# Second mixture of a fused attention and two-mixture kernel: the third token tile of each expert gathered and transposed as full 128 rows, its transposes in one run behind the first down products, the matmul order written out

## The chip, the cores and the metric

The kernel runs on one core of a Trainium2 chip. The metric is device microseconds (us) of one execution; lower is better.

## The reference

Attention over 2 x 8 heads of 576 tokens gives x (1152 tokens by 512). A first mixture of 8 experts weighs every expert for every token. The second mixture, where the change is, sends each token to its two best experts:

```python
def _moe2_ref(x, w_gate, w_noise, noise, w1, w2):
    noisy_logits = x @ w_gate + np.log1p(np.exp(x @ w_noise)) * noise
    top2 = np.argpartition(-noisy_logits, 2, axis=1)[:, :2]
    ...                       # top2_w: softmax over the two
    for e in range(E):        # E = 8, D = 512, F = 1024
        for k in range(2):
            mask = top2[:, k] == e
            h = np.maximum(x[mask] @ w1[e], 0.0)
            out[mask] += top2_w[mask, k, None] * (h @ w2[e])
```

## The kernel before

Every fp32 operand of a large product is split into a rounded high part and a low rest (`split`: ScalarE writes the high part, VectorE the rest), and each product is three matmuls (`mm3`, L164): high by high, high by low, low by high.

Routing on the chip writes, for each expert, a table of token rows. Expert 0 is handled within the routing code. The other seven are ordered by how many tokens they got, and `expert(i)` for i = 0 to 6 takes the i-th. It has room for CAPS[i] = 344, 320, 312, 304, 298, 292, 288 tokens: two tiles of 128 and a third of 88, 64, 56, 48, 42, 36, 32 rows (`sizes`). Table slots that no token took hold the numbers of the zero rows ahead of the tokens. Above that room a branch at the end would take the rest; it isn't taken here.

In `expert(i)`, in program order:

- `fetch(i + 1)`: three gathers of the next expert's token rows from HBM, one per tile, by indirect DMAs of GpSimd (`pull`, L563), into five buffers `xg`.
- `up`: for each of 8 blocks of hidden units 12 matmuls into a PSUM tile `h` (L164, in the traces h<-xh,wh and the like, as wide as the expert's room; 96 in all), then `split` into `hh` and `hl`. Where the third tile has at most 64 rows (i = 1 to 6, "short"), its hidden values go unsplit into `tail`.
- Loading and converting the weights: both halves of this expert's w2 (`vs`: the first into a `wh`/`wl` buffer, the second into `xwh`/`xwl`), both halves of the next expert's w1 (`ws`). The buffers `wh`/`wl` are three. For a short expert the raw w2 lies in `acc`.
- `prep`: the next expert's tokens are transposed on TensorE (L750, `xgt<-cs,xg`). There are four steps, one per quarter of the 512 features; a step transposes a 128-feature block of all three tiles side by side into one PSUM tile of tag "b" (two buffers), and `split` moves it to `xh` and `xl` (ACT L104, DVE L106). The third tile's transpose takes k rows of `xg` and k rows and columns of the unit matrix.
- The down products: `part(j, h)` of the class `Down` is tile j by half h of w2: 12 matmuls `y<-wh,hh` and the like, 512 wide (L164). A tile's two parts add up in one PSUM tile of tag "a" or "c"; after part 1 ScalarE scales it (L820), and GpSimd adds it to the output by an indirect DMA (L824). For a short expert the third tile goes through `tail` (L838): unsplit fp32 matmuls `y<-acc,tail` that put pieces of the output side by side in the PSUM partitions. In the traces each of them is two records, 32 in all for i = 1 to 5.

For expert(0) to expert(5) the scheduler of the kernel's language chooses where TensorE's instructions stand (it keeps what depends on each other in order). Expert 0, the routing and expert(6) stand under `manual_schedule`, so that TensorE takes them as they are written. ScalarE, VectorE and the queues are scheduled by the language in all of expert(0) to expert(6).

The tokens of expert(0) are transposed at the end of the routing code by the same `prep_steps`, a step after every sixth matmul of expert 0's last tile (`between`, `down(vs, [late], ...)`).

Of the kernel before, what the change touches and what calls it, by code (L numbers as in the profile page):

```python
# [19 lines left out]
N, DM, E, F = B * S, H * D, 8, 1024  # L20
# [42 lines left out]
def tile_kernel(ctx: ExitStack, tc: tile.TileContext, qL, kL, vL, qS, kS, vS, wg, u12, w1, w2, wgn, noise, v1, v2, cst, masks, dummy, out):  # L63
    nc = tc.nc
# [9 lines left out]
    def ps(tag, name):  # L74
        return psum.tile([128, 512], F32, tag=tag, name=name)
# [9 lines left out]
    ident = cs[:, C_ID:C_ID + 128]  # L85
# [13 lines left out]
    def split(hi, lo, src, relu=False):  # L99
        if relu:  # L100
            seen[0] = nc.scalar.activation(hi, src, AF.Relu)  # L101
            nc.vector.scalar_tensor_tensor(lo, src, 0.0, hi.bitcast(F32), op0=ALU.max, op1=ALU.subtract)  # L102
        else:
            seen[0] = nc.scalar.activation(hi, src, AF.Copy)  # L104
            firsts.append(seen[0])
            nc.vector.tensor_tensor(lo, src, hi.bitcast(F32), op=ALU.subtract)  # L106

    def fetch_w(src, raw=None):
        if raw is None:
            raw = rpool.tile([128, 4, 512], F32, tag="raw", name="raw")  # L110
        nc.sync.dma_start(raw, src)
        return raw

    def conv_w(raw, spare=False, pool=False):
        if spare:
            hi, lo = (xpool.tile([128, 4, 512], F32R, tag=t, name=t, bufs=1) for t in ("xwh", "xwl"))
        else:
            hi, lo = (wpool.tile([128, 4, 512], F32R, tag=t, name=t, bufs=3) for t in ("wh", "wl"))
        if pool:
            for s in range(4):  # L120
                nc.scalar.activation(hi[:, s], raw[:, s], AF.Copy)
                nc.gpsimd.tensor_tensor(lo[:, s], raw[:, s], hi[:, s].bitcast(F32), op=ALU.subtract)
            return hi, lo
        for s in range(2):
            split(hi[:, 2 * s:2 * s + 2], lo[:, 2 * s:2 * s + 2], raw[:, 2 * s:2 * s + 2])
        return hi, lo

    def load_w(src, spare=False):
        return conv_w(fetch_w(src), spare)
# [6 lines left out]
    def conv_u2(raw):  # L136
        hi, lo = (upool.tile([128, 2, 512], F32R, tag=t, name=t) for t in ("u2h", "u2l"))
        split(hi, lo, raw)
        return hi, lo

    def conv_u1(raw):
        hi, lo = (upool.tile([128, 7, 2, 128], F32R, tag=t, name=t) for t in ("u1h", "u1l"))
        v = raw.rearrange("p c (j n) -> p j c n", j=2)
        for j in range(2):
            split(hi[:, 2 * j:2 * j + 2].rearrange("p a b n -> p (a b) n"),
                  lo[:, 2 * j:2 * j + 2].rearrange("p a b n -> p (a b) n"), v[:, j])
        return [[[x[:, 2 * j + c // 2, c % 2] for c in range(NC)] for j in range(2)] for x in (hi, lo)]

    def conv_wino(raw):
        hi, lo = (upool.tile([128, 7, 2, 128], F32R, tag=t, name=t) for t in ("u1h", "u1l"))  # L150
        t = upool.tile([128, 4, 2, 128], F32, tag="ut", name="ut", bufs=1)
        b11, b21, b12, b22 = (raw[:, 2 * k:2 * k + 2, j * 128:(j + 1) * 128] for j in range(2) for k in range(2))
        for o, x, y in ((0, b12, b11), (2, b22, b12), (1, b22, t[:, 0]), (3, b21, t[:, 1])):
            nc.gpsimd.tensor_tensor(t[:, o], x, y, op=ALU.subtract)  # L154
        split(hi[:, :2].rearrange("p a b n -> p (a b) n"), lo[:, :2].rearrange("p a b n -> p (a b) n"), raw[:, :, :128])
        split(hi[:, 2], lo[:, 2], b22)
        split(hi[:, 3:], lo[:, 3:], t)
        return hi, lo
# [389 lines left out]
    def total(m=None):  # L548
        p = ps("b", "cnt")
        nc.tensor.matmul(p[:, :E], onesb, cnt, start=True, stop=m is None)  # L550
        if m is not None:
            for i in range(RB):
                nc.tensor.matmul(p[:, :E], onesb, m[:, i], start=False, stop=i == RB - 1)
        return p

    def gather(row, n, rows=PAD + N):
        tt = gpool.tile([128, 2], I32, tag="tt", name="tt", bufs=3)
        nc.sync.dma_start(tt[:n], table[ds(row, n), :])
        return tt, pull(tt, n, rows)

    def pull(tt, n, rows=PAD + N):
        xg = gpool.tile([128, DM], F32, tag="xg", name="xg", bufs=5)
        nc.gpsimd.indirect_dma_start(out=xg[:n], out_offset=None, in_=x2d[:rows, :],  # L563
                                     in_offset=bass.IndirectOffsetOnAxis(ap=tt[:n, 0:1], axis=0))
        return xg
# [31 lines left out]
    for q in range(NP):  # L597
        raw = fetch_u(0, q)
        with tc.issue_after(firsts[min(q, 1) * 3 + 8].ins):
            a, b = conv_u1(raw[0]), conv_u2(raw[1])  # L600
# [28 lines left out]
    for q in range(NP):  # L629
        q = NP - 1 - q  # L630
        if q < NP - 1:
            raw = fetch_u(0, q)
            a, b = conv_u1(raw[0]), conv_u2(raw[1])
# [73 lines left out]
    for e in range(1, E - 1):  # L707
        for q in range(NP):
            raw = fetch_u(e, q)
            a, b = conv_wino(raw[0]), conv_u2(raw[1])  # L710
            for u in range(2):
                x = Unit(a, u)
# [30 lines left out]
    def prep_steps(xgs, ns, c0, bank="b"):  # L743
        n = sum(ns)

        def step(c):
            p = ps(bank, "xgt")
            o = 0
            for xg, k in zip(xgs, ns):
                nc.tensor.transpose(p[:, o:o + k], xg[:k, c * 128:(c + 1) * 128], ident[:k, :k])  # L750
                o += k
            split(xh[:, c, c0:c0 + n], xl[:, c, c0:c0 + n], p[:, :n])

        return [partial(step, c) for c in range(NC)]

    def prep(xgs, ns, c0):
        for step in prep_steps(xgs, ns, c0):
            step()

    def hid(x, f, o, n):  # L760
# [85 lines left out]
    def down(ws, tts, ns, o, last=False):  # L846
        d = Down(ws, tts, ns, o)
        order = [(j, h) for j in range(len(ns)) for h in range(2)]
        if not last:
            order.sort(key=lambda x: x[1])  # L850
        for j, h in order:
            d.part(j, h)
# [5 lines left out]
    def sizes(i):  # L858
        return 128, 128, CAPS[i] - FULL
# [8 lines left out]

    def fetch(i):
        tts = [lists[i][:, j] for j in range(3)]  # L870
        return [(t, pull(t, k)) for t, k in zip(tts, sizes(i))]

    def weights(w, e, h):
        return w[ds(e, 1), h].rearrange("o p c n -> (o p) c n")
# [47 lines left out]
    raws = fetch_w(w1[0, 1]), fetch_w(w2[0, 1])  # L922
    ORDERED = {mybir.EngineType.PE, mybir.EngineType.DVE, mybir.EngineType.Activation}
    with tc.manual_schedule(engines=ORDERED):
# [6 lines left out]
        raws = [fetch_w(v1[0, h]) for h in range(2)]  # L931
# [32 lines left out]
        got = [gather(o, 128, PAD + 768) for o in range(0, EARLY, 128)]  # L964
        g2(*b0, (6, 7), e, False)
        p = total()
# [3 lines left out]
        ws = [conv_w(raws[0])]  # L970
# [3 lines left out]
        raws = [fetch_w(v2[0, h]) for h in range(2)]  # L974
# [7 lines left out]
        vs = [conv_w(raws[0])]  # L982
# [14 lines left out]
        raws = [fetch_w(weights(v1, order[0], 0))]  # L997
# [17 lines left out]
        ws = new  # L1015
# [4 lines left out]
        got = got1  # L1020
# [6 lines left out]
    def expert(i, ws, got):  # L1027
        n, last = CAPS[i], i == E - 2
        k = n - FULL
        short = k <= 64  # L1030
        cur = got
        if not last:
            got = fetch(i + 1)
        tail = gpool.tile([128, 8, 64], F32, tag="tail", name="tail") if short else None
        up(ws, (i + 1) % 3 * 384, 0, n, banks="dac", tail=tail)
        raws = [fetch_w(weights(v2, order[i], h), acc[:, 4 * h:4 * h + 4] if short else None) for h in range(2)]
        vs = [conv_w(raws[0]), conv_w(raws[1], True)]
        if not last:
            ws = [load_w(weights(v1, order[i + 1], h)) for h in range(2)]
            prep([x for _, x in got], sizes(i + 1), (i + 2) % 3 * 384)  # L1040
        tts = [t for t, _ in cur]
        if not short:
            down(vs, tts, sizes(i), 0, last)
            return ws, got
        d = Down(vs, tts[:2], (128, 128), 0)
        d.part(0, 0)
        d.part(1, 0)
        d.tail(raws, tail, tts[2], k)
        d.part(0, 1)
        d.part(1, 1)  # L1050
        return ws, got

    for i in range(E - 2):
        ws, got = expert(i, ws, got)
    most = nc.values_load(bigi, min_val=0, max_val=4 * ROWS)
    with tc.manual_schedule(engines={mybir.EngineType.PE}):
        expert(E - 2, ws, got)

    with tc.If(most > 0):
        with tc.For_i(0, E, 1) as e:  # L1060
            begin = nc.values_load(ovr[:1, ds(e, 1)], engines=(mybir.EngineType.SP,), min_val=0, max_val=E * ROWS - NOVER * OVER)
            with tc.For_i(0, NOVER, 1) as r:
                tt, xg = gather(begin + r * OVER, OVER)
                prep([xg], [OVER], 0)
                ws = [load_w(weights(w, e, h)) for w in (v1, v2) for h in range(2)]
                up(ws[:2], 0, 0, OVER)
                down(ws[2:], [tt], [OVER], 0)
# [82 lines left out]
```

## Time and profile before

| | |
|---|---|
| time, median of 3 runs | 1117.54 us (1116.22 to 1119.85) |
| profiled execution: its own time, the span | 1120.2 us |
| TensorE matmuls busy | 1102.6 us, 98% of the span |
| VectorE / ScalarE / GpSimd busy | 665.0 / 394.3 / 173.8 us |
| start of expert(0) to expert(6) in the chain that ended last | 892.39 us |

For the profiled execution the span is the one time that is listed; nothing is listed around it. A matmul's record lasts longer than its share of TensorE, since matmuls overlap. A busy share of 98% therefore does not say that the engine runs at its best rate. That is read from the starts, or from the chain of work that ended last, whose pieces follow each other without a gap.

### The profile page before, as it was taken

Reading aid. Unit: us, or ns where it says so; the run is one execution under the profiler, and the core shown is the slowest. Engines: PE = TensorE matmul, PEld = TensorE weight load, DVE = VectorE, ACT = ScalarE, POOL = GpSimd, SP = SyncE. Lnnn points to the kernel's source line nnn. Section 1 sums busy time; section 2 is a strip of 40 time slices with the busy share of each in tenths; the row PEclk is TensorE's granted clock in tenths of the full one; section 3 lists DMA queues with packets and bytes.
Section 4 is the critical chain, followed back from the end, with each engine's and each line's share of the span. In section 5 each row is a group of like instructions: output and inputs, shape, how many; then the busy total and the mean of one; then the engine's idle time right before and its main releaser. Section 6 shows DMA issues by size and latency. Waiting matters only on the chain.

```text
span 1120.2 us, 17350 instructions
## 1 busy us (share of the span) xinstructions
PE 1102.6 (98%) x6878; PEld 957.3 (85%) x6878; DVE 665.0 (59%) x1374; ACT 394.3 (35%) x884; POOL 173.8 (16%) x204
## 2 busy tenths in 40 slices
PE   9899999999999999999999999999999999999996
PEld 5677989899998999899999989998888888888885
DVE  5785697666666666666666767553366364544440
ACT  5542144333332333323333323231123263544441
POOL 2110022111112111121111110000041431322211
PEclk9899999999999999999999999999999999999999
DMA  9512135112111121111111111022113682555541
GB/s 278 151 57 75 38 103 159 38 38 75 39 38 38 39 76 38 38 39 38 45 69 38 38 39 56 20 75 75 47 49 88 174 303 41 197 196 194 170 102 23
DMA packets 31216, 96.27 MB, mean 86 GB/s; under 512 B 6522, under 2 KB 15226, under 8 KB 22556
## 3 DMA queue, kind: packets, MB, share of 16 engines
q1 hardware_dynamic: 16028, 78.13, 20.6%
q0 software_dynamic: 5200, 10.17, 4.3%
q10 hardware_dynamic: 9904, 6.83, 2.0%
q8 instruction: 55, 0.90, 0.3%
q14 instruction: 29, 0.24, 0.1%
HBM read 83.60 MB, written 11.60 MB: 85 GB/s over the span
## 4 chain that ended last, share of the span: by engine, by line
PE 87%; DVE 4%; issue 3%; DMA 3%; POOL 2%; ACT 1%; POOLq 0%; ACTq 0%; SPq 0%
PE y L164 40%; PE h L164 16%; PE a L665 14%; PE b L665 7%; PE d L665 3%; PE y L838 2%; PE xgt L750 1%; DMA table<-en,si 1%; PE sc L225 1%; POOL table L498 1%; PE sc L210 1%; PE tr L241 1%; DMA wg_sb<-in_wg 1%; PE ot L247 1%; DMA xg<-x2d,tt 1%
## 5 line engine op out<-in xcount | busy, mean ns | idle before, releaser
L591 DVE SCALAR_TENSOR_TENSOR acc<-y,P,acc 128x512 f32<-128x512 f32 x207 | 152.6, 748 | 141.7 <-PE y L164 141.7
L164 PE MATMUL y<-u2h,gh 128*128 128x512 f32 x504 | 198.3, 394 | 0.3 <-DVE acc L591 0.3
L164 PE MATMUL y<-u2l,gh 128*128 128x512 f32 x504 | 197.1, 391 | 0.0
L164 PE MATMUL y<-u2h,gl 128*128 128x512 f32 x504 | 189.9, 392 | 0.7 <-DVE gl L102 0.6
L154 POOL TENSOR_TENSOR ut<-raw 128x256 f32<-128x256 f32 x48 | 35.6, 762 | 513.2 <-DVE u1l L106 442.0
L164 PEld LDWEIGHTS y<-u2h,gl 128*128 128x128 f32 x504 | 94.3, 188 | 20.9 <-DVE gl L102 2.0
L164 PE MATMUL h<-xl,wh 128*128 128x384 f32 (+8 forms) x352 | 110.2, 313 | 0.0
L164 PE MATMUL h<-xh,wh 128*128 128x384 f32 (+8 forms) x352 | 109.6, 315 | 0.3 <-DVE hl L102 0.3
L164 PE MATMUL h<-xh,wl 128*128 128x384 f32 (+8 forms) x352 | 109.8, 312 | 0.0
L164 PEld LDWEIGHTS y<-u2h,gh 128*128 128x128 f32 x504 | 94.7, 188 | 15.4 <-issue 0.7
L164 PEld LDWEIGHTS y<-u2l,gh 128*128 128x128 f32 x504 | 94.6, 188 | 13.9
L101 ACT ACTIVATE hh<-h 128x256 fp32r<-128x256 f32 (+2 forms) x88 | 35.5, 415 | 97.8 <-PE h L164 97.7
L164 PEld LDWEIGHTS h<-xh,wh 128*128 128x128 f32 x352 | 66.2, 189 | 2.1 <-DVE hl L102 0.6
L164 PEld LDWEIGHTS h<-xl,wh 128*128 128x128 f32 x352 | 66.4, 189 | 1.1 <-issue 0.6
L104 ACT ACTIVATE u2h<-raw 128x1024 fp32r<-128x1024 f32 x31 | 32.8, 1059 | 96.2 <-PE y L164 96.2
L164 PEld LDWEIGHTS h<-xh,wl 128*128 128x128 f32 x352 | 66.3, 188 | 0.0
L102 DVE SCALAR_TENSOR_TENSOR hl<-h,hh 128x256 fp32r<-128x256 f32 (+2 forms) x88 | 40.4, 464 | 38.9 <-ACT hh L101 38.9
L106 DVE TENSOR_TENSOR wl<-raw,wh 128x1024 fp32r<-128x1024 f32 x42 | 49.6, 1221 | 18.7 <-ACT wh L104 18.7
L665 PE MATMUL b<-sh,u1h 128*128 128x288 f32 x192 | 56.9, 296 | 0.0
L665 PE MATMUL a<-sh,u1l 128*128 128x288 f32 x192 | 56.9, 296 | 0.0
L665 PE MATMUL b<-sl,u1h 128*128 128x288 f32 x192 | 56.8, 296 | 0.0
L665 PE MATMUL a<-sl,u1h 128*128 128x288 f32 x192 | 56.7, 295 | 0.0
(248 smaller groups left out, 2502.5 us busy)
## 6 DMA issues: line engine op xcount, KB each, us to landing
raw<-in_u SPq DMA_DIRECT2D x31, 1024.0 KB, 5.0
raw<-in_v SPq DMA_DIRECT2D x20, 1024.0 KB, 10.3
acc<-in_v SPq DMA_DIRECT2D x12, 1024.0 KB, 7.5
raw<-in_w SPq DMA_DIRECT2D x4, 1024.0 KB, 5.3
out<-zero ACTq DMA_DIRECT2D x1, 3072.0 KB, 18.7
x2d<-acc ACTq DMA_DIRECT2D x9, 256.0 KB, 2.0
vs<-in_vL SPq DMA_DIRECT2D x4, 432.0 KB, 11.4
ks<-in_kS SPq DMA_DIRECT2D x4, 297.0 KB, 7.7
```

The costliest lines, as they stand in the source:

```text
L101: seen[0] = nc.scalar.activation(hi, src, AF.Relu)
L102: nc.vector.scalar_tensor_tensor(lo, src, 0.0, hi.bitcast(F32), op0=ALU.max, op1=ALU.subtract)
L104: seen[0] = nc.scalar.activation(hi, src, AF.Copy)
L106: nc.vector.tensor_tensor(lo, src, hi.bitcast(F32), op=ALU.subtract)
L154: nc.gpsimd.tensor_tensor(t[:, o], x, y, op=ALU.subtract)
L164: nc.tensor.matmul(o, a, b, start=start, stop=stop)
L210: nc.tensor.matmul(o, onesb, onesb[:, None, :].to_broadcast([128, 4, 128]), start=True, stop=True)
L225: nc.tensor.matmul(sc[h * 64:h * 64 + w, i * nk:(i + 1) * nk], qs[r, j * w:(j + 1) * w], ks[r, j * step:j * step + nk], start=False, stop= ...
L241: nc.tensor.transpose(tr[:nk, i * nq:(i + 1) * nq], s[:, i], ident[:nq, :nq])
L591: nc.vector.scalar_tensor_tensor(acc[:, t], p, P[:, t, scale:scale + 1], acc[:, t], op0=ALU.mult, op1=ALU.add)
L665: nc.tensor.matmul(p, l[:, b, c], m, start=first and i == 0, stop=i == 5, skip_group_check=not first)
L838: nc.tensor.matmul(p[j * w:j * w + k, :d], hr[:, f, :k], raws[f // 4][:, f % 4, j * d:(j + 1) * d], start=f == 0, stop=f == 7)
```

## The change

Each expert now gathers 128 rows for its third tile and transposes all of them; of the transposed columns only the first k are split and used, as before. Expert(0) to expert(5) stand in written order on TensorE too. In `expert`, `prep` comes behind the first down part, with its four quarters in PSUM tags b, b, d, d, so that twelve transposes stand in a row; behind them comes `tail` for a short expert, then the other parts. Expert(6), which prepares nothing, has `tail` behind its first part instead of its second.

```diff
         def step(c):
-            p = ps(bank, "xgt")
+            p = ps(bank[c % len(bank)], "xgt")
             o = 0
             for xg, k in zip(xgs, ns):
-                nc.tensor.transpose(p[:, o:o + k], xg[:k, c * 128:(c + 1) * 128], ident[:k, :k])
+                nc.tensor.transpose(p[:, o:o + 128], xg[:, c * 128:(c + 1) * 128], ident)
                 o += k
...
-    def prep(xgs, ns, c0):
-        for step in prep_steps(xgs, ns, c0):
+    def prep(xgs, ns, c0, bank="b"):
+        for step in prep_steps(xgs, ns, c0, bank):
...
-        return [(t, pull(t, k)) for t, k in zip(tts, sizes(i))]
+        return [(t, pull(t, 128)) for t in tts]
...
-            prep([x for _, x in got], sizes(i + 1), (i + 2) % 3 * 384)
         tts = [t for t, _ in cur]
-        if not short:
-            down(vs, tts, sizes(i), 0, last)
-            return ws, got
-        d = Down(vs, tts[:2], (128, 128), 0)
+        d = Down(vs, tts[:2] if short else tts, sizes(i)[:2 if short else 3], 0)
         d.part(0, 0)
-        d.part(1, 0)
-        d.tail(raws, tail, tts[2], k)
-        d.part(0, 1)
-        d.part(1, 1)
+        if not last:
+            prep([x for _, x in got], sizes(i + 1), (i + 2) % 3 * 384, "bbdd")
+        if short:
+            d.tail(raws, tail, tts[2], k)
+        for j in range(1, len(d.ns)):
+            d.part(j, 0)
+        for j in range(len(d.ns)):
+            d.part(j, 1)
         return ws, got
 
-    for i in range(E - 2):
-        ws, got = expert(i, ws, got)
+    with tc.manual_schedule(engines={mybir.EngineType.PE}):
+        for i in range(E - 2):
+            ws, got = expert(i, ws, got)
```

On TensorE, in expert(1) of the kernel before, the scheduler had put two quarters of `prep` between `up` and the down products:

```order
L164 MATMUL h<-xh,wl 128x320
L750 MATMUL xgt<-cs,xg 128x128 x2
L750 MATMUL xgt<-cs,xg 128x56
L750 MATMUL xgt<-cs,xg 128x128 x2
L750 MATMUL xgt<-cs,xg 128x56
L164 MATMUL y<-wh,hh 128x512
```

The other two quarters stood in the middle of its `tail`, ahead of the parts with `xwh`:

```order
L164 MATMUL y<-wh,hl 128x512
L838 MATMUL y<-acc,tail 64x256 x8
L750 MATMUL xgt<-cs,xg 128x128 x2
L750 MATMUL xgt<-cs,xg 128x56
L750 MATMUL xgt<-cs,xg 128x128 x2
L750 MATMUL xgt<-cs,xg 128x56
L838 MATMUL y<-acc,tail 64x256 x8
L164 MATMUL y<-xwh,hh 128x512
```

In the changed kernel the same stretch of expert(1) has all twelve transposes in one row, behind the twelve matmuls of part(0, 0) and directly ahead of the undivided tail:

```order
L164 MATMUL y<-wh,hh 128x512
L164 MATMUL y<-wl,hh 128x512
L164 MATMUL y<-wh,hl 128x512
L750 MATMUL xgt<-cs,xg 128x128 x12
L838 MATMUL y<-acc,tail 64x256 x16
L164 MATMUL y<-wh,hh 128x512
```

At the head of expert(0), before the change, the scheduler had filled TensorE behind the third and fourth quarter of the tokens' transposes with matmuls of several hidden blocks (`h`), so that the fourth quarter (the last `xgt`) was not needed soon:

```order
L164 MATMUL h<-xh,wh 128x344
L750 MATMUL xgt<-cs,xg 128x128 x2
L750 MATMUL xgt<-cs,xg 128x88
L164 MATMUL h<-xl,wh 128x344
L164 MATMUL h<-xh,wl 128x344
L164 MATMUL h<-xl,wh 128x344
L164 MATMUL h<-xh,wl 128x344
L164 MATMUL h<-xl,wh 128x344
L164 MATMUL h<-xh,wl 128x344
L164 MATMUL h<-xh,wh 128x344 x3
```

In the changed kernel the first hidden block follows in written order. Behind the last `xgt` stand the rest of the second quarter (two matmuls), the third quarter (three), and then the fourth, which reads what those transposes gave:

```order
L164 MATMUL h<-xh,wh 128x344
L750 MATMUL xgt<-cs,xg 128x128 x3
L164 MATMUL h<-xl,wh 128x344
L164 MATMUL h<-xh,wl 128x344
L164 MATMUL h<-xh,wh 128x344
L164 MATMUL h<-xl,wh 128x344
L164 MATMUL h<-xh,wl 128x344
L164 MATMUL h<-xh,wh 128x344
L164 MATMUL h<-xl,wh 128x344
```

## Rows read from the trace of the kernel before

**Rows 1.** First part of the page: busy us, share, instructions.

```profile
PE 1102.6 (98%) x6878; PEld 957.3 (85%) x6878; DVE 665.0 (59%) x1374; ACT 394.3 (35%) x884; POOL 173.8 (16%) x204
```

**Rows 2.** Chain that ended last, 928 us on: start us, us, piece.

```profile
943.06 0.98 PE xgt L750 x6
944.04 5.79 PE y L164 x24
949.83 1.88 PE y L838 x16
951.71 1.13 PE xgt L750 x6
952.84 1.88 PE y L838 x16
954.72 5.78 PE y L164 x24
960.49 13.83 PE h L164 x96
...
983.40 0.57 PE y L838 x2
...
985.09 3.59 PE y L838 x30
...
1097.26 5.60 PE y L164 x24
```

**Rows 3.** Windows of expert(1) to expert(5): length, busy (x), PEclk, DMA share, GB/s.

```profile
943.06:960.49 17.43, 17.43 (x94) 12.46 (x93) 6.77 (x10) 7.31 (x12) 4.68 (x5) 1.00 0.44 160
...
1067.15:1084.46 17.31, 17.31 (x94) 12.07 (x93) 6.80 (x10) 7.25 (x12) 2.16 (x2) 1.00 0.37 126
sum 87.68, PE 87.68 PEld 61.72 DVE 29.43 ACT 32.51 POOL 19.16; mean PE 17.54 PEld 12.34 DVE 5.89 ACT 6.50 POOL 3.83
```

**Rows 4.** Timeline of TensorE's weight loads (PEld), 943 us: start, us, [idle before].

```profile
943.20 0.40 PEld L750 LDWEIGHTS xgt<-cs,xg 56*128 56x128 f32 x3 [0.17 <-issue]
943.77 0.14 PEld L750 LDWEIGHTS xgt<-cs,xg 56*128 56x128 f32 x1 [0.17 <-issue]
```

**Rows 5.** Chain that ended last, 885 to 930 us.

```profile
882.01 6.88 DMA xg<-x2d,tt
...
890.66 0.30 PE xgt L750 x3
890.95 1.43 PE y L164 x6
...
896.00 9.95 PE h L164 x62
...
928.97 1.03 PE h L164 x7
```

**Rows 6.** Timeline of PE, 845 us: four transposes of the routing.

```profile
845.37 0.60 PE L401 MATMUL x2t<-cs,acc 128*128 128x128 f32 x4
845.72 0.48 PE L164 MATMUL y<-xwh,hh 128*128 128x512 f32 x1
```

**Rows 7.** Instructions on tile xgt: durations ns, minimum/median/maximum.

```profile
L750 PE MATMUL xgt<-cs,xg x92: 241/272/330, 846.5 to 1076.6; 128*128 128x128 f32 x64, 88*128 88x88 f32 x4, 64*128 64x64 f32 x4, 56*128 56x56 f32 x4
L104 ACT ACTIVATE xh<-xgt x32: 379/420/459, 847.1 to 1076.9; 128x256 fp32r<-128x256 f32 x4, 128x344 fp32r<-128x344 f32 x4, 128x320 fp32r<-128x320 f32 x4, 128x312 fp32r<-128x312 f32 x4
L106 DVE TENSOR_TENSOR xl<-xgt,xh x32: 423/466/518, 847.5 to 1077.3; 128x256 fp32r<-128x256 f32 x4, 128x344 fp32r<-128x344 f32 x4, 128x320 fp32r<-128x320 f32 x4, 128x312 fp32r<-128x312 f32 x4
```

**Rows 8.** DMA issues from 879.3 to 880 us: KB each, median us to landing.

```profile
xg<-x2d,tt POOLq DMA_INDIRECT x1, 5.2
```

**Rows 9.** Waits from 905 us on: total us, times, longest.

```profile
ACT wh L104 <- DMA acc<-in_v: 7.6, 5, 2.4
```

**Rows 10.** Stretches by window, columns as in the third group.

```profile
983.40:988.60 5.20, 5.20 (x39) 2.86 (x38) 0.95 (x2) 0.85 (x2) 2.90 (x3) 1.00 0.25 43
43.20:53.30 10.10, 10.02 (x66) 6.67 (x68) 6.94 (x19) 5.88 (x18) 1.16 (x3) 0.50 0.30 100
```

## The prediction

> **What bounds the kernel now.** I read the page's busy shares first: TensorE is busy 98% of the span [rows 1]. That does not say that it cannot be faster, so I went on to the chain of work that ended last. From expert(1) on, and up to the last expert's parts, it runs through TensorE alone: up (h), transposes (xgt), parts (y), tail (y L838), piece after piece [rows 2]. The reader should see that no other engine ends a wait there. So what TensorE's own order costs is paid in full, and what ScalarE, VectorE and the queues do is free as long as it is on time. Then I cut the stretch between the end of one up and the start of the next: 17.43 us for expert(1), 87.68 us for five experts together [rows 3]. All that the change moves there lies in that stretch; up itself keeps its 96 matmuls.
>
> **Where the transposes lose time.** In expert(1) six transposes take 0.98 us and 1.13 us [rows 2], some 0.16 to 0.19 us each. At the head of expert(0) three of the same kind take 0.30 us [rows 5], and four of the routing's go from 845.37 to 845.72 [rows 6], 0.09 us each. What differs is the third tile: 88 rows there, 128 in the routing, 56 rows in expert(1). The weight loads show it. At the 56-row transpose, and again behind it, the loader sits idle 0.17 us and is not ahead of the matmuls [rows 4]. A change between full and half height of the array stops that overlap. Each pass through a quarter pays it twice.
>
> **Part by part, expert(1) to expert(5).** I build the new stretch from chain pieces.
> - Matmuls y: 24 behind an up took 5.60 us [rows 2], 0.233 us each. Twelve ahead of the transposes: 2.80 us.
> - Twelve full transposes behind y: three take 0.30 us, and the six y behind them 1.43 us instead of 1.40 [rows 5], so 0.11 us each with the exit: 1.32 us. The 0.09 of [rows 6] would give 1.1. I take the former, since it has the exit in it.
> - Tail undivided. In expert(2) it was cut into 0.57 us (2 records) and 3.59 us (30) [rows 2]. The 30 are the rest of the first block's matmul (two records by itself) and seven blocks of two matmuls side by side. That makes 16 steps, as many as eight whole blocks need. So 3.59 us, against 1.88 + 1.88 for two halves. The entry from a transpose is in it.
> - The other 36 y: 24 behind a tail took 5.78 us [rows 2], 0.18 above 5.60; with 12 more at 0.233: 8.58 us.
>
> Sum 16.29 us. Before, the mean was 87.68 / 5 = 17.54 us, so 1.25 us an expert and 6.2 us for five. This has three sources: no partial transposes, one pass through the transposes instead of two, and no break in the tail.
>
> **Expert(0).** From its second transposed quarter (890.66) to the next up (928.97) it took 38.31 us [rows 5]. New: nine transposes for itself at 0.11 us, 0.99; twelve y of the routing's last tile, 2.80; 96 h at 9.95 / 62 = 0.16 us, 15.41; 72 y, 16.78; twelve transposes for expert(1), 1.32. Together 37.30 us. Against it stands one new wait. In the order behind the last transpose, the fourth quarter's second matmul, which needs the rest xl, comes after six matmuls h, or 0.97 us. The rest is there after a matmul (0.27), ScalarE's copy (0.46 for this widest tile) and VectorE's (0.52) [rows 7], 1.25 us and some 0.1 us of signals. So 0.4 us are lost, between 0 and the whole 1.35 us. I take 0.4: gain 0.6 us.
>
> **What is hidden.**
> - The bigger gathers. The 88-row one took 6.88 us to land [rows 5], a 128-row one 5.2 us [rows 8], so rows do not set it. From expert(1)'s transposes on, a gather has most of an expert's time. Only the one of the head of expert(0) is waited for: it stands in the chain itself [rows 5]. There I bound it by 0 and by 40 / 88 of its 6.88 us, 3.1 us, and take 0, since the longer row is the smaller gather.
> - The four copies in a row, 4 x 0.42 us on ScalarE and 4 x 0.47 us on VectorE [rows 7]. They are needed at the next up, over 12 us of tail and y later. If that cover were gone, a wait as at expert(0) would cost 0.4 us each time.
> - PSUM. Tag d lends its two buffers to the third and fourth quarter. Their last users are the fourth and seventh hidden blocks, copied out before the twelve y are through.
> - The first half of w2, whose buffer part(1, 0) now frees after the tail. In the old order, the next conversion waited for its transfer into `acc` instead, 7.6 us in five waits [rows 9]. That transfer starts when the tail has read `acc`, now some 4 us earlier (2.80 + 1.32 + 3.59 us behind the up, instead of 11.66). If this cover were gone, the conversion would be late by about 4 us, with an up of 13 us ahead of its use. So nothing.
> - Expert(6) keeps as many entries to and exits from its tail. Its last part and scatter stay last: 0.
>
> **Sum.** 6.2 + 0.6 = 6.8 us less of 1120.2 us, 1113.4 us in the profiled execution, or 0.61%. The median of the runs shown is 1117.54, 0.24% below the span, so 1110.7 us.
>
> **A rule against this change.** Twelve transposes and the tail make a stretch of 4.9 us without a split product. In expert(2) such a stretch of 5.20 us (tail, transposes, tail) ran at a granted clock of 1.00, the 2.4 GHz level [rows 10]. The Trainium skill ("TensorE: Matmul & The Clock Gate", Part 4: PE-mode transpose) says that transposes do not count as busy for the clock gate in the way other matmuls do, and gives about 275 ns for one in a kernel. By the trace's clock in the stretch the sum stays as it is; by the rule the first two rivals below come about. The 272 ns of our row is a duration [rows 7], and starts are 0.09 to 0.11 us apart.
>
> **The rivals.**
> 1. *The clock falls behind the row of transposes* (slower). Place: the parts behind it, in six experts. Only six transposes stood together before, and half of the 5.20 us stretch was their neighbours. Price: the one low stretch in the trace where TensorE kept working is 10.10 us at 0.50 [rows 10], the 1.2 GHz level, and costs at most half its length, 5 us. Six of them would be 30 us less the 6.8: 1141 us. It decides from two experts in six on. Against it: the 5.20 us row; and the low stretch lies in the attention, at 43 us, among other work. Chance 3%.
> 2. *Transposes in a long row come at their duration*, 0.272 us. Twelve are 3.26 us instead of 1.32, six times: 11.6 us less the gain of 6.8, 1122 us (slower). The fours and threes speak against it [rows 5, 6]. Chance 3%.
> 3. *Full rows don't help:* the idle loads come from something else in the run. Then twelve take 0.98 + 1.13 us as before, 0.79 more than I reckon, in six experts: the gain is 6.8 - 4.7 = 2.1 us, 1115.4 us (same). The 88-row threes speak against it. Chance 6%.
> 4. *The head of expert(0) gives the gain back:* the larger first gather lands up to 3.1 us later, and the copies behind the last quarter are exposed whole, 0.95 us more than reckoned. The gain is then 2.75 us: 1114.8 us (same). Chance 7%.
>
> **Chances and range.** The forecast has 81%: all terms are durations of this trace, and the order is fixed. About 0.3% (3.4 us) is what a measurement can tell from no change. Rivals 3 and 4 lie inside that, 1 and 2 above it. Faster 0.81, same 0.13, slower 0.06. The forecast's own range is 1107.5 to 1113.5: transposes by 0.09 us give 1.3 us more, expert(0) without a wait 0.4 more, both copies and gather in part 1.5 less, and medians move by some 1.5 us. Toward the other cases I go up to 1116.5, which takes in rivals 3 and 4; 1107 stays the low end.
>
> **What would show it.** In the profile after: twelve transposes in one chain piece of 1.2 to 1.4 us and no idle loads between them (if not, rival 3 or 2); tail of 32 records in one piece of 3.6 us; stretches between ups of 16.3 us; PEclk 1.00 in them (if not, rival 1); a wait of about 0.4 us ahead of an early h of expert(0); at 888 us the same wait for the gather. The prediction is wrong if a wait on a copy or a transfer stands ahead of an up or a tail.

## The result, and the profile after

| | before | after |
|---|---|---|
| first comparison, median | 1119.85 us (1116.22 to 1125.7, 7 executions) | 1110.57 us (1108.08 to 1114.08, 7) |
| ratio, 95% interval | | 0.9906 [0.9883, 0.993] |
| second comparison ("after again" below), median | 1118.81 us (1115.7 to 1131.94, 17) | 1112.26 us (1108.7 to 1115.75, 12) |
| ratio, 95% interval | | 0.9938 [0.9914, 0.9962] |
| profiled execution: span, mean granted clock | 1120.2 us, 0.993 | 1108.8 us, 0.997 |

The kernel became faster, by 0.6 to 0.9%. The forecast was 1110.7 us against 1117.54, a ratio of 0.9939.

The first part of the page, as in [rows 1]: matmuls are busy 10.9 us less, in as many instructions. (Some 5 us of that are not the change's, as shown below.)

```profile
PE 1091.7 (98%) x6878; PEld 954.6 (86%) x6878; DVE 664.3 (60%) x1374; ACT 394.4 (36%) x884; POOL 173.2 (16%) x204
```

The chain that ended last, from expert(1)'s parts on (start us, us, piece), which answers to [rows 2]:

```profile
938.17 2.80 PE y L164 x12
940.97 1.31 PE xgt L750 x12
942.28 3.60 PE y L838 x32
945.88 8.60 PE y L164 x36
954.48 13.83 PE h L164 x96
```

Four pieces stand between the ups where six stood. The next view is that of the windows between the ups, as in [rows 3]: the length of each, the busy time of PE, PEld, DVE, ACT and POOL, then the granted clock.

```profile
938.17:954.48 16.31, 16.31 (x94) 12.50 (x94) 6.22 (x10) 7.21 (x12) 4.43 (x4) 1.00 0.58 204
...
1056.85:1073.14 16.29, 16.29 (x95) 12.14 (x94) 6.62 (x10) 7.22 (x12) 2.99 (x2) 1.00 0.42 134
sum 81.49, PE 81.49 PEld 61.54 DVE 32.85 ACT 36.09 POOL 21.69; mean PE 16.30 PEld 12.31 DVE 6.57 ACT 7.22 POOL 4.34
```

Expert(1) to expert(5) are alike now. The sum went from 87.68 to 81.49 us, 6.19 less, at a clock of 1.00 throughout. The weight loads of expert(1)'s twelve transposes, which answer to [rows 4], are one unbroken row, with no idle time in brackets:

```profile
940.57 1.47 PEld L750 LDWEIGHTS xgt<-cs,xg 128*128 128x128 f32 x12
```

The head of expert(0) in the chain, as in [rows 5]:

```profile
884.74 0.33 PE xgt L750
885.06 1.40 PE y L164 x6
886.46 0.33 PE xgt L750 x3
...
890.53 0.34 PE xgt L750 x3
...
890.90 0.47 ACT xh L104
...
891.39 0.53 DVE xl L106
...
891.96 14.03 PE h L164 x86
...
924.08 6.02 PE h L164 x41
```

ScalarE's and VectorE's copies of the last quarter stand in the chain: this is the new wait that the prediction spoke of. From the second quarter (886.46) to the next up (924.08) it is 37.62 us, where it was 38.31.

**Where the 11.4 us between the two spans come from.** Each trace is cut at two matmuls that are the same in both: the last row of L797 transposes, ahead of TensorE's first changed instruction, and the first h of expert(1). Up to the former it is 885.44 us before and 880.48 after: 4.96 us that cannot be the change's. The trace before has them in the attention. Of 30 to 60 us (columns as above) it shows a clock of 0.83, and the trace after 1.00:

```profile
30.00:60.00 30.00, 26.55 (x257) 19.34 (x253) 21.65 (x57) 16.45 (x64) 5.55 (x12) 0.83 0.46 132
```

```profile
30.00:60.00 30.00, 28.22 (x317) 20.88 (x314) 25.66 (x70) 20.02 (x80) 7.50 (x14) 1.00 0.44 134
```

From L797 to the first h of expert(1) it is 43.37 and 43.43 us, no gain. From there to the end it is 191.34 and 184.86, 6.48 us. The change's gain inside the head is hidden by a longer wait of TensorE for the third tile's gather ahead of it, which the experiments take apart. In brackets, before and after, is the idle time of TensorE and what ended it:

```profile
888.93 0.30 PE L750 MATMUL xgt<-cs,xg 88*128 88x88 f32 x1 [0.98 <-DMA xg<-x2d,tt]
```

```profile
884.74 0.33 PE L750 MATMUL xgt<-cs,xg 128*128 128x128 f32 x1 [1.75 <-DMA xg<-x2d,tt]
```

### The profile page after: what moved, and what is told of

Same layout as the page of the kernel before. It is cut to its first block, busy times and chain, and to the rows that moved or that the text cites. A ratio compares the mean times of both kernels' runs of the same rounds, so it can differ in the third digit from the quotient of the medians.

```text
span 1108.8 us, 17357 instructions
## 1 busy us (share of the span) xinstructions
PE 1091.7 (98%) x6878; PEld 954.6 (86%) x6878; DVE 664.3 (60%) x1374; ACT 394.4 (36%) x884; POOL 173.2 (16%) x204
## 4 chain that ended last, share of the span: by engine, by line
PE 87%; DVE 3%; issue 3%; DMA 3%; POOL 2%; ACT 1%; POOLq 0%; ACTq 0%; SPq 0%
PE y L164 40%; PE h L164 16%; PE a L665 14%; PE b L665 7%; PE d L665 3%; PE y L838 2%; DMA table<-en,si 1%; POOL table L498 1%; PE sc L210 1%; PE sc L225 1%; PE tr L241 1%; PE xgt L750 1%; DMA wg_sb<-in_wg 1%; PE ot L247 1%; DMA xg<-x2d,tt 1%
```

## The experiments

The runs came in three groups, each on one chip beside the kernel before (median 1122.63 us in the first, 1118.81 in the second, 1118.98 in the third). "Stretches" is the sum of the five windows of [rows 3]. "Head" is the time from the last L797 transposes to the first h of expert(1).

| run | median us | ratio [95%] | stretches us | head us |
|---|---|---|---|---|
| before, first trace | | | 87.68 | 43.37 |
| before again | 1122.51 | 1.0005 [0.9976, 1.0034] | 87.69 | 45.93 |
| full rows only | 1115.4 | 0.9936 [0.9911, 0.9962] | 83.69 | 45.25 |
| order only | 1121.74 | 0.999 [0.9964, 1.0016] | 85.21 | 46.73 |
| late steps | 1113.53 | 0.9914 [0.9888, 0.994] | | 40.78 |
| after, first trace | | 0.9906 [0.9883, 0.993] | 81.49 | 43.43 |
| after again | 1112.26 | 0.9938 [0.9914, 0.9962] | | 44.90 |
| late steps again | 1108.22 | 0.9896 [0.9857, 0.9935] | | 41.12 |
| later steps | 1107.45 | 0.9886 [0.9847, 0.9925] | 81.48 | 42.34 |
| 72 rows | 1110.53 (one) | | 80.65 | 44.90 |
| later steps, 72 rows | 1107.6 | 0.9896 [0.9864, 0.9928] | | 41.81 |
| double row | 1119.99 | 1.0005 [0.9983, 1.0028] | 88.05 | 48.63 |
| before, later steps | 1115.19 | 0.9972 [0.9951, 0.9994] | | 41.84 |

### The kernel before, again

No edit.

> The kernel before, unchanged, timed against itself. In the two profiles the changed kernel stands 5.0 us ahead already at 825 us, before its first changed instruction, and there the profile of before has 10.2 us at half clock in the attention. Theory (those 5 us are chance between executions and no part of the change): ratio 1.000 within 0.3%, mean clocks of the executions between 0.993 and 0.998, and executions with a clock near 0.997 are some 5 us shorter than those near 0.993. Rival (the old program always falls to half clock there, so the change is worth all of it): all clocks near 0.993.

The attention ran at a granted clock of 1.00 this time, and the last L797 transposes came at 880.73 us, as in the changed kernel, not at 885.44. So the 4.96 us ahead of the change belong to an execution and not to a kernel. The executions without a trace fit that: of the twelve, the four with a mean granted clock of 0.991 took 1125.7 to 1129.3 us, the five with 0.995 or more 1119.6 to 1122.4. But the head took 45.93 us in place of 43.37, in the same code. The timeline of TensorE (in brackets: idle time, and what ended it) shows why:

```profile
885.23 0.30 PE L750 MATMUL xgt<-cs,xg 88*128 88x88 f32 x1 [1.99 <-DMA xg<-x2d,tt]
885.32 0.65 PE L164 MATMUL y<-wh,hh 128*128 128x512 f32 x1
885.77 0.63 PE L164 MATMUL y<-wl,hh 128*128 128x512 f32 x1
```

TensorE comes to the transposes of the third tile 1.99 us before its gather has landed. The y behind it then start 0.45 us apart (885.32, 885.77), where 0.233 is usual. The windows before, during and behind that give the clock (1.00, 0.53, 1.00):

```profile
882.00:885.30 3.30, 1.24 (x7) 0.52 (x6) 2.13 (x13) 0.72 (x3) 2.69 (x3) 1.00 1.03 294
885.30:888.90 3.60, 3.60 (x11) 2.88 (x12) 0.52 (x1) 0.64 (x2) 0.59 (x1) 0.53 0.83 176
888.90:892.00 3.10, 3.10 (x18) 2.66 (x17) 0.80 (x2) 0.73 (x2) 0.00 (x0) 1.00 0.03 6
```

So the wait for the gather is paid again behind it: 3.6 us at a clock of 0.53, nearly the 1.2 GHz level, cost about 1.7 us more (3.6 x 0.47).

### The full rows alone

The kernel before, its order untouched:

```diff
-                nc.tensor.transpose(p[:, o:o + k], xg[:k, c * 128:(c + 1) * 128], ident[:k, :k])
+                nc.tensor.transpose(p[:, o:o + 128], xg[:, c * 128:(c + 1) * 128], ident)
...
-        return [(t, pull(t, k)) for t, k in zip(tts, sizes(i))]
+        return [(t, pull(t, 128)) for t in tts]
```

> Full 128 rows gathered and transposed, in the order of before. Theory (three sources: full rows, one pass instead of two, undivided tail): a pass of six falls from 0.98 to 0.7 us behind an up and from 1.13 to 0.8 us in a tail, so the five stretches between ups fall from 87.68 to 84.6 us; expert(0) gains 0.6 us, its wait for the first gather grows by up to 0.8 us as in the changed kernel; in all some 3 us or 0.3% faster. Rival (the row count is everything): the stretches fall to 81.6 us as in the changed kernel, 0.55% faster.

The chain from expert(1)'s parts, and the sum of the five windows:

```profile
939.79 0.65 PE xgt L750 x6
940.45 5.59 PE y L164 x24
946.04 1.88 PE y L838 x16
947.92 0.80 PE xgt L750 x6
948.72 1.88 PE y L838 x16
950.60 5.78 PE y L164 x24
```

```profile
sum 83.69, PE 83.69 PEld 61.13 DVE 30.30 ACT 31.90 POOL 18.89; mean PE 16.74 PEld 12.23 DVE 6.06 ACT 6.38 POOL 3.78
```

Six transposes take 0.65 and 0.80 us in place of 0.98 and 1.13, and the 24 y behind them 5.59 in place of 5.79. The last is what the theory had left out: a 56-row transpose also cost 0.20 us at the exit to the next full matmul. The sum fell by 4.0 us. That is the larger part of the gain, more than the theory gave the rows and less than the rival did. The median came out better than that (7.2 us), and why stays open. By times alone the rows would be the whole gain, 0.9936 here and 0.9938 for the whole change in the second comparison; what the order adds is seen only in the stretches.

### The order alone

The changed kernel with the two lines above put back to k rows.

> The new order, twelve transposes in a row and the tail behind them, with the third tile's k rows as before. Theory: twelve cost about 2.1 us instead of 1.31, so the five stretches take 85.4 us against 87.68 before and 81.6 in the changed kernel; expert(0) gains nothing net and keeps a wait of 0.5 us behind its last transpose; in all 2 us or 0.2% faster. Rival (the row count is everything, the order nothing): stretches of 87.7 us and no gain.

The chain of the same place, and one row of the weight loads inside the twelve:

```profile
942.83 2.80 PE y L164 x12
945.62 2.11 PE xgt L750 x12
947.73 3.60 PE y L838 x32
951.34 8.59 PE y L164 x36
```

```profile
946.34 0.40 PEld L750 LDWEIGHTS xgt<-cs,xg 56*128 56x128 f32 x3 [0.17 <-issue]
```

Twelve partial transposes in one row take 2.11 us, exactly the 0.98 + 1.13 of two passes [rows 2]: one row in place of two saves nothing in the transposes, since the loader sits idle ahead of each 56-row tile here too (a row begins with the 56-row load and holds the two of 128 that follow). What the order saves is outside them: 0.16 us of tail (3.60 in place of 1.88 + 1.88) and 0.18 us of y (2.80 + 8.59 in place of 5.79 + 5.78), 0.33 us in this expert and 2.47 over the five (85.21 us). Expert(2) and expert(4), whose tail was cut behind its first two records (0.57 and 3.59 us in the former), gained 0.75 and 0.76 us. The median doesn't tell this from no gain: 0.999, with an interval from 0.9964 to 1.0016, and a head of 46.73 us behind a wait of 2.40. Rows and order together would be 6.46 us by their sum; the changed kernel has 6.19. Both remove the same exit into y (0.18 to 0.20 us an expert), while full tiles gain 0.14 more in one row (1.31 in place of 0.65 + 0.80).

### 72 rows

The changed kernel with tiles of 72 rows (88 for expert(0)):

```diff
-                nc.tensor.transpose(p[:, o:o + 128], xg[:, c * 128:(c + 1) * 128], ident)
+                nc.tensor.transpose(p[:, o:o + max(k, 72)], xg[:max(k, 72), c * 128:(c + 1) * 128], ident[:max(k, 72), :max(k, 72)])
...
-        return [(t, pull(t, 128)) for t in tts]
+        return [(t, pull(t, max(k, 72))) for t, k in zip(tts, sizes(i))]
```

> The changed kernel, but third tiles gathered and transposed as 72 rows (88 for expert(0)) in place of 128. Theory: what costs time is a transpose over at most 64 rows, behind which the weight loader sits idle; 72 rows are free of it. Then twelve transposes take 1.2 to 1.4 us, as with 128, and stretches between ups 16.2 to 16.4 us. Rival: any partial tile stalls: then 2.0 to 2.1 us for twelve, as in the order alone, and 17.1 us.

The piece of the chain, and the loads, without idle time:

```profile
941.44 1.14 PE xgt L750 x12
```

```profile
941.28 1.11 PEld L750 LDWEIGHTS xgt<-cs,xg 128*128 128x128 f32 x11
```

So what stalls the loader here is not a tile that is partial, but one of 64, 56 or fewer rows: 72 and 88 rows are free of it, and twelve transposes with 72 are cheaper than with 128 (1.14 us in place of 1.31). Rows and columns of the short tile were widened together, so that which of the two counts isn't separated. Rows alone are not the whole of it: in the changed kernel the loader is idle 0.17 us ahead of expert(1)'s tail too (942.21), whose loads have 128 rows and 64 columns.

The Trainium skill ("TensorEngine Tiling (Array Packing)", Key Properties) says that a change of the array's tiling mode drains TensorE. The trace agrees with that, if tiles of at most 64 rows are loaded in another mode than those of 72; the mode itself stands in no row here. What it cost is 0.20 us for each short tile, there and back: (2.11 - 1.31) / 4.

### The double row

The transposes of expert(0) to expert(5) done twice, 24 in a row, the result the same:

```diff
-            for xg, k in zip(xgs, ns):
-                nc.tensor.transpose(p[:, o:o + 128], xg[:, c * 128:(c + 1) * 128], ident)
-                o += k
+            for again in range(2 if len(bank) > 1 else 1):
+                o = 0
+                for xg, k in zip(xgs, ns):
+                    nc.tensor.transpose(p[:, o:o + 128], xg[:, c * 128:(c + 1) * 128], ident)
+                    o += k
```

> The changed kernel with every transpose of the rows in expert(0) to expert(5) done twice: 24 in a row in place of 12, the same result. Theory: a full transpose costs its start, 0.102 to 0.11 us, however many stand together: 24 take 2.5 to 2.65 us, the stretch between ups 17.5 to 17.6 us, the granted clock stays 1.00 behind them, and the kernel is 7.3 to 8 us longer than the changed one, ratio 1.000 to 1.001 against the kernel before. Rival, the clock falls behind a long row: parts behind the row at a clock near 0.5, and the stretches above 18 us, up to 22. Rival, a long row comes at the duration of a transpose, 0.272 us: 24 take 6.5 us.

Windows of expert(1): the 24 transposes, the tail, the other parts; the clock is the third number from the end.

```profile
944.18:946.80 2.62, 2.62 (x26) 2.45 (x26) 2.12 (x6) 1.29 (x3) 0.00 (x0) 1.00 0.00 0
946.80:950.40 3.60, 3.60 (x34) 2.21 (x33) 0.81 (x2) 0.43 (x1) 2.93 (x3) 1.00 0.39 96
950.40:959.00 8.60, 8.60 (x39) 6.95 (x39) 2.05 (x2) 3.64 (x5) 1.64 (x3) 1.00 0.99 356
```

24 take 2.62 us, twice 1.31, and 6.2 us of transposes and tail leave the clock at 1.00 behind them. The five stretches grew by 6.56 us, 1.31 each, and the ratio went back to 1.0005. This refutes the first two rivals in this kernel. The rule weighed in the prediction (the Trainium skill, "TensorE: Matmul & The Clock Gate", Part 4: PE-mode transpose), by which transposes do not count as busy in the way other matmuls do, had no effect here: a transpose started every 0.11 us, and no row of 24 brought the clock down. Whether a longer row would isn't tested.

### The steps of the head, later

Of the eight traces with the steps in their old place, seven show TensorE waiting 1.6 to 2.4 us for a gather at the head; only the first trace of before has 1.0. In that one the last L797 transposes started 3.4 us behind the issue of the third tile's gather, in six others 2.3 us, and in that of the double row, where a second wait of 1.53 us follows one of 2.34, 1.0 us. This edit of the changed kernel leaves the gather fifteen matmuls of time in place of six, with the quarters in tags b, b, d, d; "later steps" has 15 in place of 13:

```diff
-        for step in prep_steps([x for _, x in got], sizes(0), 384):
-            between.extend((None, None, None, None, None, step))
+        between.extend([None] * 13)
+        for step in prep_steps([x for _, x in got], sizes(0), 384, "bbdd"):
+            between.extend((None, step))
```

> The changed kernel, with the four transposing steps of expert(0) behind the 15th, 17th, 19th and 21st matmul of the routing's last tile instead of the 6th, 12th, 18th and 24th, in tags b, b, d, d. Theory (the head of expert(0) loses 1.9 us to the first gather and 0.5 us to the last quarter's copies, both because of where the steps stand): both waits go, the first matmul h of expert(1) comes 2.2 to 2.5 us earlier counted from the routing's first transposes of hidden rows, 0.2% faster than the changed kernel, 0.75 to 0.95% faster than before. Rival (the wait moves along, since the gathers land when transfers of weights let them): no gain.

> The changed kernel with the four transposing steps of expert 0's last tile behind the 15th, 17th, 19th and 21st matmul, beside the changed kernel itself on one chip. Theory: the wait for the first gather goes (it came 3.9 to 4.5 us behind the last L797 transposes, where the step stood 1.7 us behind them), and with it the stretch of 3.4 us at half clock that three traces show behind it: 2 to 3 us less than the changed kernel, ratio 0.997 to 0.998 against it. Rival: the profiled execution was a lucky one, and the wait is only moved behind more matmuls in most executions: then it stands within 1 us of the changed kernel.

> The same with the steps behind the 17th, 19th, 21st and 23rd matmul: 0.47 us more room for the gather. Theory: as the 15th, within 0.5 us, if the gather is there by the 15th matmul; up to 0.5 us better if it often is not. Rival: with one matmul behind the last step the copies of the last quarters come too late for the first hidden block, and a wait of 0.3 to 1 us stands ahead of an early h.

For comparison the changed kernel ran again beside them, on the chip of the second group.

> The changed kernel again, beside the kernel before on another chip. Theory: what the change itself gives stands behind the first up of expert(1), 6.5 us by the two traces (191.34 to 184.86 us up to the end), and the rest of the 11.4 us between the two profiled executions is chance of the attention's clock and of the wait for the first gather. Then the ratio is the product of the two halves measured alone, 0.9936 x 0.999 = 0.9926, within 0.991 to 0.995. Rival: the change also changes the head or the attention for good; then 0.9906 comes again, and 0.990 or less is as likely as 0.991. The head, from the matmul behind the last transpose of hidden rows (L797) to the first up of expert(1), took 43.1 us in the changed kernel's trace; theory: 43 to 46.5, according to whether the wait for the gather is followed by a stretch at half clock.

Its timeline at the same place, and the windows behind it (clock 0.50, then 0.99):

```profile
883.39 0.35 PE L750 MATMUL xgt<-cs,xg 128*128 128x128 f32 x1 [1.64 <-DMA xg<-x2d,tt]
883.48 0.69 PE L164 MATMUL y<-wh,hh 128*128 128x512 f32 x1
883.97 0.63 PE L164 MATMUL y<-wl,hh 128*128 128x512 f32 x1
```

```profile
883.80:886.90 3.10, 3.10 (x10) 2.41 (x10) 0.52 (x1) 0.43 (x1) 0.49 (x1) 0.50 0.97 226
886.90:892.00 5.10, 5.10 (x29) 4.33 (x27) 1.40 (x3) 1.77 (x4) 0.84 (x1) 0.99 0.02 4
```

The same kernel, which had come through its head at a clock of 1.00 in the first trace, lost 1.5 us here; its ratio, 0.9938, lies in the range that the theory gave (0.991 to 0.995, 0.9926 in the middle). With the steps behind the 15th matmul neither trace shows a wait for the gather. The trace of the later steps, behind the 17th, shows one of 0.99 us, where L797 stood only 1.0 us behind the gather's issue, with the next y at the usual pace (an exit of 0.32 us, duration 0.40, where half the clock gave 0.63):

```profile
886.10 0.33 PE L750 MATMUL xgt<-cs,xg 128*128 128x128 f32 x1 [0.99 <-DMA xg<-x2d,tt]
886.19 0.48 PE L164 MATMUL y<-xwh,hl 128*128 128x512 f32 x1
886.51 0.40 PE L164 MATMUL y<-xwh,hh 128*128 128x512 f32 x1
```

On one chip the medians are 1112.26, 1108.22 and 1107.45 us. The heads of the three traces, 44.90, 41.12 and 42.34, account for 3.8 and 2.6 of the 4.0 and 4.8 us, which is more than the 2 to 3 us of the theory. The executions without a trace agree: all twelve of the two late kernels had a mean granted clock of 0.997 or more, of the changed kernel's twelve beside them three. That 17th is better than 15th isn't shown: 0.8 us between medians, against intervals of some 4 us to either side. In the one trace of the 17th its rival came in part: the last quarter's copies stand in the chain, directly ahead of the first h (ScalarE 0.47 us at 888.07, VectorE 0.53 at 888.56, h at 889.13).

> The kernel before with only the four steps of expert 0's last tile moved behind the 17th, 19th, 21st and 23rd matmul; nothing of the change. Theory: what the later steps give does not depend on the change: the wait for the first gather and the half clock behind it cost the kernel before as much, 2 to 5 us, ratio 0.995 to 0.998. Rival: they cost only the changed kernel, since it comes to the head sooner: ratio 0.999 to 1.001.

The same edit in the kernel before (with `bank[c % len(bank)]`, which the tags need) gave 0.9972 [0.9951, 0.9994] and a head of 41.84 us without a wait for the gather. The mean granted clock was 0.997 or more in eleven of its twelve executions, and in eleven of 23 of the kernel before beside it. So the wait is not the change's work.

> The two edits that did better, together: steps behind the 17th, 19th, 21st and 23rd matmul, third tiles of 72 rows (88 for expert(0)). Theory: they lie in different places and add: the 72 rows gave twelve transposes in 1.14 us in place of 1.31 at six places, 1.0 us, so that the ratio is 0.9886 less 0.0009, 0.988, within 0.985 to 0.991. Rival: the smaller gather or the narrower transposes give something back at the head, and it stands at 0.989 to 0.990.

Both edits together gave 0.9896 and 1107.6 us, no better than the later steps alone in what can be measured. That lies in the theory's range and in the rival's too. In the trace the twelve transposes take 1.14 us at each place, as expected, but expert(5)'s up went from 12.80 to 13.02 us, as it was in the kernel before, which gives 0.22 of 1.0 us back. Why that up has two lengths stays open. 12.80 us stands with full rows and with the order alone, 13.02 with 72 rows in both kernels that had them.

## Why the prediction was right, point by point

- **The stretch.** Right in every term: 2.80 us of y (2.80 forecast), 1.31 of transposes (1.32), 3.60 of tail (3.59), 8.60 of y (8.58). The mean is 16.30 us against 16.29, and the five gave 6.19 against 6.2.
- **Three sources.** Partly right. Of "no partial transposes, one pass through the transposes instead of two, and no break in the tail", the first is the largest (4.0 of 6.19 us by itself) and the third is as reckoned. The second is small: twelve partial transposes took the same 2.11 us in one row as in two passes, and twelve full ones 1.31 in place of 1.45.
- **"A change between full and half height".** Supported: it is the rows at or below 64 that stall, not those short of 128. But [rows 4] was misread. Its first row holds three loads, the 56-row one and the next quarter's two of 128; so both 0.17 us stand ahead of a 56-row load, and none "again behind it". Behind one the loader's records show 0.06 us idle. "Pays it twice" is right for the matmuls all the same: in expert(1) their starts are 0.20 us apart from a full tile to the short one and 0.20 back, 0.11 between full ones. The terms of the sum came from chain pieces, and the misreading entered none.
- **Expert(0).** From the second quarter on, 37.62 us against 37.30 + 0.4; the gain is 0.69 against 0.6. In the new wait the second matmul of the fourth quarter starts at 891.96 us, 0.47 behind its neighbour in place of 0.16, and the next 0.27 behind: 0.42 us, where 0.4 was forecast.
- **The first gather.** That the larger gather lands no later is right: it took 6.40 to 7.14 us for 88 rows in six traces, 6.42 to 7.59 for 128 in five. What the prediction missed is that this wait is no fixed number: 0.98 us in the trace it was read from, 1.6 to 2.4 in the seven others with the early steps, and in all of these but one a stretch near half clock behind it. The trace of before happened to have TensorE late against the gather (3.4 us behind its issue, in place of 2.3) and so a short wait. The term was right at 0 as a difference between kernels, and it is where some 4 us were still to be had.
- **Hidden.** Right in its result. The conversions of w2 wait longer for `acc` than in [rows 9], not shorter: 17.5 us in five waits, the longest 4.6. That is idle time of ScalarE, which comes to them sooner; they start no later. In expert(1) the one on `acc` started 13.4 us behind the end of the up (951.55), before 14.1 (957.20). None of them is in the chain from expert(1) on.

```profile
ACT wh L104 <- DMA acc<-in_v: 17.5, 5, 4.6
```

- **The sum.** 6.48 us behind the first h of expert(1) (the stretches' 6.19, 0.22 of expert(5)'s up, which was not forecast, and 0.07 of rest) and 0.69 in expert(0) make 7.2 us, where 6.8 was forecast. That is a ratio of 0.9936 on 1120.2 us. The second comparison agrees with it (0.9938). The first, 0.9906, is better by 2 to 3 us than the change accounts for in the traces. So it is in part luck that its median, 1110.57 us, stands 0.13 us from the forecast: the kernel before had 1119.85 there and not 1117.54. Two things fit it. One is executions of before with the low clock in the attention, as in the profiled one. The other is on record: six of the changed kernel's seven executions had a mean granted clock of 0.997 or more, as in its first trace, which had no half clock at the head, but only three of twelve in the second comparison. Only one execution of each has a trace, and so neither is shown.
- **The rivals.** The clock's fall and the long row: refuted by the double row, for rows of up to 24. "Full rows don't help": refuted by the rows alone. The head that gives the gain back: the copies were exposed by 0.42 us, not whole.

## What to carry to other kernels

Look at the loader's idle time where a tile is short: here it was idle 0.17 us ahead of each tile of 64 rows and fewer among full ones, each such tile cost 0.20 us, and padding to 72 rows removed that, as padding to 128 did. Sum the pieces of the chain, not the engine's busy time; where TensorE was alone in the chain the sum came true to 0.1 us a stretch. Before you price a wait on TensorE from one trace, take a second trace of the same kernel: a wait for a transfer at 1.0 us in one execution was 2 us and 1.7 us of half clock in the next, and moving the consumer nine to eleven matmuls later gave another 4.0 to 4.8 us by the medians, more than half of the 6.6 us of the whole change.

## What the runs showed that was not expected

- A wait of TensorE for a transfer can cost more than its length. In six of the seven traces with waits of 1.6 us and more at the head a stretch near half clock followed; behind those of 1.64, 1.99 and 2.37 us it was 3.1 to 3.6 us at a granted clock of 0.50 to 0.53. A wait of 1.75 us in the changed kernel's first trace had none behind it, nor had those of 0.98 and 0.99 us; so in this range the wait's length alone does not decide. The Trainium skill ("TensorE: Matmul & The Clock Gate", HAM oscillation — how this bites in real kernels) tells of a loop whose waits for data bring the clock down for the work that comes next. These rows agree in that, with shorter waits than those of its loop.
- A 56-row transpose cost 0.20 us once more at the exit to a matmul 512 wide (5.79 us for the 24 behind it, against 5.59 behind a full one).
- A 72-row tile was transposed faster than a 128-row one among full ones: twelve in 1.14 against 1.31 us, 0.04 us for each third tile.
